# Issue order inside a pooled attention and a gated two-layer product: what is queued behind what, on VectorE, TensorE and the DMA queue

## The chip, the cores and the metric

The kernel runs on one core of one Trainium2 chip. The metric is the device time of one execution in microseconds. The core has a matrix engine (TensorE; PE in the profile, its weight loads are PEld), VectorE (DVE), ScalarE (ACT), GpSimd (POOL) and SyncE (SP), which in this kernel issues nearly all DMAs. Each engine works through its own instructions in the order in which they stand in the program.

## The reference, cut to what matters

```python
# q, k, v: 8 batches x 8 heads x 576 tokens x 64;  w_in: 512 x 2048;  w_out: 2048 x 512; all float32
k_p = k.reshape(B, H, 72, 8, D).mean(axis=3)          # eight keys become one
v_p = v.reshape(B, H, 72, 8, D).mean(axis=3)
scores = q @ k_p.T / sqrt(D)
attn = exp(scores - max(scores))                      # softmax over 72 pooled keys
attn = attn / (attn.sum(-1) + 1e-9)
x = (attn @ v_p), heads side by side                  # 4608 tokens x 512
h = x @ w_in                                          # 4608 x 2048
g = h * clip(h + 3, 0, 6) / 6
out = g @ w_out                                       # 4608 x 512
```

## The kernel before, in words

**Precision.** Products are made in a fast 32-bit format. Each operand is split into a high part (a copy into that format, by ScalarE) and a low part (the rest, a subtraction by VectorE), and each product is three matmuls: high by high, high by low, low by high.

**Blocks.** The 4608 tokens are cut into blocks of 512, 256 and ten times 384. The first four blocks run plainly (`Step`): for each of 16 slices f of the middle dimension, `h()` makes twelve matmuls (line 813), ScalarE and VectorE make the gate and its two parts (lines 821 to 833), and `out()` multiplies them with `w_out` two steps later (line 843). In VectorE's work on a step the last instruction is `lo()` (line 833).

**Super blocks.** The other eight blocks are taken in pairs by `super_block`, four in all. Its first half makes h for two blocks at once with seven products in the place of eight. `N1` lists 56 operations (pair i of slices, product o from 1 to 7), six matmuls of 384 columns each (line 1041). Each reads a pre-added piece of `w_in`, streamed from DRAM in chunks of two operations into a ring of four (`next_w`, tile ws, line 938), and a pre-added part of x: x1 to x7, made by `x_ops` of four quarters of x (b11, b21 of the first block, b12, b22 of the second). Results of one pair gather in the PSUM banks X, Y and Z; between products ScalarE keeps a copy (`keep`, line 1019), VectorE adds (`plus`, line 1014), and `gate` follows (lines 1008 and 1009). The last operation of a pair (o = 4) needs the sum that `plus` takes after o = 7 from the same bank. The second half makes out: for 16 slices f, `split_g` makes the two parts of g (lines 1025 and 1026) and six token tiles t take three matmuls each (line 1086), with `w_out` streamed slice by slice into a ring of four (`next_w2`, tile ws2, line 944; the profile calls both rings ws, this one from w2d). The sums of t = 0 to 5 stand in the banks o0, h0, o2, o1, h1, o3; all but o3 also serve the h half, and o3 is one of three that the attention uses meanwhile.

**The sources of both streams** are written by the kernel while blocks 2 and 3 run: `sums_of` adds quarters of `w_in` (line 909, then lines 914 to 916) in one buffer and stores them (line 918); `plain_of` stores what needs no addition through `store` (line 921, 24 stores of 256 KB and 16 of 512 KB).

**Attention** for later blocks is cut into steps that are dealt out among the products (`Paced.slot`). `scores` (lines 443 to 485) makes one tile's scores for four heads and divides them on GpSimd into a tile a (line 479); `transposes` (lines 549 to 572) turns it round; `av` (lines 619 to 621) multiplies it with the pooled values and writes x. `block_steps` puts the transposes of a tile behind the scores of `TLAG` = 3 later ones; tile a has two buffers. Side steps load k and v for a later batch and sum over eight keys (lines 243 and 362, reductions on VectorE). A super block deals out the attention of the two blocks after next, 36% of the steps in its first half and the rest in its second, up to f = 10; from f = 11 the steps of `x_ops` follow, in the order in which `x_ops` returns them.

**Order.** All instructions are first written down in program order. Up to the fourth step of block 1 the order on each engine is then set by hand (`ORDER`; `window` holds both ends of that stretch). Behind it a planner decides: it goes through a model of the machine and gives each engine, among the instructions that are ready there, the one that was written down first. An edge made by `behind(a, b)` costs no semaphore on the chip; it only keeps the planner from placing a before b. `after_products`, the only such edge of this kind before, names as b the last TensorE instruction written down so far, and is called behind the reductions of k and v, the two additions of line 909, the stores of line 921 and the loads of ws2.

Of the kernel before, what the change touches and what calls it, by code (L numbers as in the profile page):

```python
# [17 lines left out]
P = 128  # L18
# [8 lines left out]
TLAG = 3  # L27
# [62 lines left out]
def attention_moe_kernel(  # L90
# [72 lines left out]

    def after_products():

        if len(window) == 2:
            behind(traced[-1], next(i for i in reversed(traced) if i.engine == mybir.EngineType.PE).name)

# [64 lines left out]
    def prep_k(b, p):  # L233

        two = b == 0
        if not two:
            ks = pool.tile([P, 1, SP], F32, name="ksum", bufs=1)
        elif p % 2 == 0:
            ks = ksum[p // 2] = piece(0, 2 * SP).rearrange("p (i s) -> p i s", i=2)
        else:  # L240
            ks = ksum[p // 2]
        i = p % 2 if two else 0
        nc.vector.tensor_reduce(
            out=ks[:, i], in_=kraw.pop((b, p)).rearrange("p (s o) -> p s o", o=POOL), axis=AX.X, op=ALU.add
        )
        after_products()
        if i == two:

            scale = 1.0 / (POOL * D**0.5)
            for h in range(2):  # L250
                rows = slice(h * D, (h + 1) * D)
                nc.scalar.mul(kbds[b % 2][rows, p - i : p + 1, h * SP : (h + 1) * SP], ks[rows], scale)
# [99 lines left out]
    def prep_v(b, p):  # L352


        if p == 0:
            if b not in W:
                place_v(b)
            sums = ring("vsum")[:, : (NPAIR + NG) * D]
            vsum[b] = sums.rearrange("p (c d) -> p c d", d=D)
        n = P if p < NPAIR else 3 * REM  # L360
        vs, st = vsum[b], vraw.pop((b, p))
        nc.vector.tensor_reduce(  # L362
            out=vs[:n, p], in_=st[:n, : POOL * D].rearrange("p (o d) -> p d o", o=POOL), axis=AX.X, op=ALU.add
        )
        after_products()
        if p == NPAIR - 1:
            place_heads(b, vs[:, :NPAIR])
        elif p == NPAIR + NG - 1:
            place_rest(b, vs[:, NPAIR:])
# [50 lines left out]
    class Scores:  # L420
# [49 lines left out]
        def divide(self, engine):  # L470

            e, sm = self.e, self.sm
            if self.a is None:
                self.a = pool.tile([P, 4 * D], F32, name="a", bufs=2)
                if self.g == 0:
                    rests[self.tile] = pool.tile([P, NG, 2 * REM], F32, name="ar", bufs=2)
                self.rest = rests[self.tile][:, self.g]
# [167 lines left out]
    def block_steps(j):  # L645
# [12 lines left out]
        for t in tiles_of[j]:  # L658
            pre = loads_behind(t)
            for g in range(NG):  # L660
                steps.append((pre, lambda t=t, g=g: scores(j, t, g), "scores", [x[0] for x in t]))
                pre = []
                todo.append((t, g))
                if len(todo) > TLAG:
                    turn()
# [134 lines left out]
    class Step:  # L800
# [30 lines left out]
        def lo(self):  # L831
            self.glo = early.tile([P, max(BLOCKS)], F32R, name="glo", bufs=3)[:, : self.n]
            nc.vector.tensor_tensor(out=self.glo, in0=self.g, in1=self.ghi.bitcast(F32), op=ALU.subtract)

        def out(self, slot=no_slot):
# [67 lines left out]
    def sums_of(i, h):  # L903
# [4 lines left out]
        for r, w in enumerate(pair_of(i)):  # L908
            nc.vector.tensor_tensor(
                out=q[:, 2 * r : 2 * r + 2], in0=w[:, 0, :, half], in1=w[:, 1, :, half], op=ALU.add  # L910
            )
            after_products()
        for to, a, b, how in ((0, 0, 2, ALU.subtract), (2, 2, 3, ALU.add), (3, 3, 0, ALU.subtract), (1, 1, 3, ALU.subtract)):
# [6 lines left out]
    def store(to, src):  # L920
        nc.sync.dma_start(to, src)
        after_products()

# [11 lines left out]
    def next_w(n):  # L935
        while (m := len(loaded)) <= n // CHUNK + AHEAD and m < len(supers) * len(w_dram):
            loaded[m] = late[0].tile([P, CHUNK, 2, 2 * P], F32R, name="ws", bufs=NSTREAM)
            nc.sync.dma_start(loaded[m].bitcast(F32), w_dram[m % len(w_dram)])
        return loaded[n // CHUNK][:, n % CHUNK]

    def next_w2(n):
        while (m := len(loaded2)) <= n + 3 and m < len(supers) * NF:
            loaded2[m] = late[1].tile([P, 2, DM], F32R, name="ws2", bufs=4)
            nc.sync.dma_start(loaded2[m].bitcast(F32), w2_dram[m % NF])
            after_products()
        return loaded2[n]
# [3 lines left out]
    def x_ops(j):  # L950
# [24 lines left out]
        def middle():  # L975
# [5 lines left out]
        return (  # L981
            mix(middle, b22, b12, ALU.subtract)
            + split(1, b11)
            + mix(b12, b12, b11, ALU.subtract)
            + split(2, b21)
            + mix(b11, b11, middle, ALU.add)
            + split(7, middle)
            + split(5, b12)
            + mix(b21, b21, b11, ALU.subtract)
            + split(6, b11)  # L990
            + split(4, b21)
            + split(3, b22)
        )

    def super_block(n, j, first_att, second_att):
# [9 lines left out]
        def gate(src, i, k):  # L1005
# [4 lines left out]
                out=g_of[i][:, k], in0=r, scalar=GSCALE, in1=src, op0=ALU.min, op1=ALU.mult  # L1010
            )

        def plus(i, k, ps, kept):
# [8 lines left out]
        def split_g(f):  # L1022
            g = g_of[f // 2][:, f % 2 :: 2]
            hi, lo = (late[1].tile([P, 2, HALF], F32R, name=m, bufs=3) for m in ("ghi2", "glo2"))
            nc.scalar.copy(hi, g)  # L1025
            nc.vector.tensor_tensor(out=lo, in0=g, in1=hi.bitcast(F32), op=ALU.subtract)  # L1026
            parts[f] = [t.rearrange("p h t -> p (h t)") for t in (hi, lo)]

        for m, (i, o) in enumerate(N1):
# [27 lines left out]
            elif o == 4:  # L1057
                gate(ps, i, 1)
        paced.upto(len(paced.steps))

# [7 lines left out]
        for f in range(NF):  # L1068
# [3 lines left out]
            for t in range(NT2):  # L1072
# [11 lines left out]
                for cols, pos in sums[t]:  # L1084
                    for k, (l, r) in enumerate(products):
                        nc.tensor.matmul(pos, l, w[:, r, cols], start=f == 0 and k == 0, stop=end and k == 2)  # L1086
                if not end:
                    continue
# [240 lines left out]
    for n, j in enumerate(supers):  # L1329
        last = n == len(supers) - 1  # L1330
        att = [] if last else att_steps(j + 2) + att_steps(j + 3)
        cut = int(0.36 * len(att))
        super_block(n, j, att[:cut], att[cut:])
# [46 lines left out]
```

## Time and profile before

| | |
|---|---|
| median of 3 runs | 915.89 us (912.76 to 915.96) |
| the profiled execution's own time | 916.45 us |
| its span, first to last instruction | 914.7 us |
| TensorE busy | 889.2 us, 97% |
| VectorE, ScalarE, GpSimd busy | 569.7, 515.6, 82.9 us |
| granted TensorE clock, mean | 0.996 |
| bytes moved by DMA | 172.63 MB, 189 GB/s on average |

The profile shows one execution. Block 0 ends and block 1 begins at about 128 us, block 2 begins at 188, block 3 at 266, and the four super blocks at 355, 500, 639 and 781 us; their second halves begin at about 417, 561, 702 and 838 us. In a timeline row the first number is the start in microseconds from the span's beginning, the second how long the merged instructions took together, and a bracket at the end gives how long the engine had been idle before and what ended that. Rows merge equal instructions (x18 is eighteen), and a row can overlap the next, since matmuls are pipelined. In a row of DMA issues the duration is that of issuing; the time to landing stands apart.

### The profile page before, as it was taken

The numbers are of one execution on the slowest core, as the hardware profiler recorded it, in microseconds if no ns is written. First come the engines' busy times: TensorE is split into PE (matmuls) and PEld (weight loads), VectorE is DVE, ScalarE is ACT, GpSimd is POOL, SyncE is SP. The second block draws the span as 40 slices with busy tenths as digits, with TensorE's granted clock in tenths as the row PEclk, the third lists the DMA queues.
The fourth block names the chain that finished last, engine by engine and source line by source line (L and its number), as shares of the span: only waits on it lengthen the run. The fifth ranks groups of instructions, "written<-read, shape, count | busy, mean of one in ns | idle before, by whom it ended". The sixth has DMA issues, their size and how long they took to land.

```text
span 914.7 us, 14060 instructions
## 1 busy us (share of the span) xinstructions
PE 889.2 (97%) x4760; PEld 797.4 (87%) x4760; DVE 569.7 (62%) x1183; ACT 515.6 (56%) x1473; POOL 82.9 (9%) x168
## 2 busy tenths in 40 slices
PE   7899999999999998999999999999999999899998
PEld 7788889998889987899888999888999888899887
DVE  5999855587876786466744845665665543744321
ACT  5898766666557565446534854554854443644221
POOL 4100002111102011000100300110200010000000
PEclk9999999999999999999999999999999999999999
DMA  9970205246659546886745666764777543576333
GB/s 292 392 270 1 79 15 160 66 155 195 210 161 340 179 144 199 287 265 204 236 162 175 231 213 215 239 200 156 235 230 224 184 127 117 197 230 217 115 121 110
DMA packets 93527, 172.63 MB, mean 189 GB/s; under 512 B 12048, under 2 KB 50704, under 8 KB 93456
## 3 DMA queue, kind: packets, MB, share of 16 engines
q1 hardware_dynamic: 93312, 171.74, 56.8%
q8 instruction: 38, 0.62, 0.3%
q14 instruction: 33, 0.27, 0.1%
q10 hardware_dynamic: 144, 0.00, 0.0%
HBM read 139.20 MB, written 32.51 MB: 188 GB/s over the span
## 4 chain that ended last, share of the span: by engine, by line
PE 86%; DVE 6%; DMA 4%; ACT 1%; SPq 1%; issue 1%; DVEq 0%; ACTq 0%
PE psx L1086 29%; PE psx L1041 24%; PE psh L813 12%; PE pso L843 12%; PE psa L619 3%; PE psa L443 3%; DMA ws<-wd 2%; PE psa L549 1%; DMA wd<-wq 1%; DMA stage<-v_l 1%; DVE x L960 1%; SPq L918 1%; PE psa L320 1%; DVE vsum L362 1%; DVE wq L916 0%
## 5 line engine op out<-in xcount | busy, mean ns | idle before, releaser
L1041 PE MATMUL psx<-x,ws 128*128 128x384 f32 x1344 | 249.4, 339 | 5.7 <-DMA ws<-wd 2.3
L1041 PEld LDWEIGHTS psx<-x,ws 128*128 128x128 f32 x1344 | 233.9, 189 | 11.5 <-ACT c L1019 2.5
L1086 PE MATMUL psx<-ws,ghi 128*128 128x512 f32 (+1 forms) x800 | 239.2, 386 | 4.8 <-DVE g L1009 2.6
L1086 PEld LDWEIGHTS psx<-ws,ghi 128*128 128x128 f32 x800 | 146.0, 188 | 31.8 <-DVE g L1009 3.5
L1086 PE MATMUL psx<-ws,glo 128*128 128x512 f32 (+1 forms) x400 | 149.0, 386 | 0.3 <-DVE glo L1026 0.3
L813 PE MATMUL psh<-xhi,w 128*128 128x384 f32 (+2 forms) x520 | 146.1, 339 | 0.3 <-DVE g L825 0.3
L843 PE MATMUL pso<-w,ghi 128*128 128x512 f32 x384 | 120.1, 399 | 0.0
L1026 DVE TENSOR_TENSOR glo<-g,ghi 128x768 fp32r<-128x768 f32 x64 | 61.5, 965 | 74.0 <-ACT ghi L1025 68.7
L813 PEld LDWEIGHTS psh<-xhi,w 128*128 128x128 f32 x520 | 93.4, 188 | 7.4 <-DVE g L825 0.5
L451 ACT ACTIVATE e<-psa,mx 128x72 f32<-128x72 f32 x256 | 78.8, 328 | 22.5 <-DVE mx L447 19.2
L1008 ACT ACTIVATE r<-g,small 128x384 f32<-128x384 f32 x96 | 55.6, 616 | 58.6 <-DVE g L1014 58.4
L1025 ACT CAST ghi<-g 128x768 fp32r<-128x768 f32 x64 | 53.1, 838 | 62.5 <-PE psx L1086 60.6
L1086 PEld LDWEIGHTS psx<-ws,glo 128*128 128x128 f32 x400 | 75.1, 188 | 14.6 <-DVE glo L1026 1.2
L813 PE MATMUL psh<-xlo,w 128*128 128x384 f32 (+2 forms) x260 | 87.3, 336 | 0.0
L479 POOL TENSOR_TENSOR a<-e,sm 128x256 f32<-128x256 f32 x60 | 41.6, 695 | 403.7 <-DVE sm L468 326.5
L843 PEld LDWEIGHTS pso<-w,ghi 128*128 128x128 f32 x384 | 68.5, 188 | 10.0
L1014 DVE TENSOR_TENSOR g<-psx,c 128x384 f32<-128x384 f32 x96 | 52.7, 554 | 35.5 <-PE psx L1041 32.8
L843 PE MATMUL pso<-w,glo 128*128 128x512 f32 x192 | 73.8, 397 | 0.0
L1019 ACT COPY c<-psx 128x384 f32<-128x384 f32 x96 | 43.4, 486 | 39.9 <-PE psx L1041 39.1
L1009 DVE SCALAR_TENSOR_TENSOR g<-r,psx 128x384 f32<-128x384 f32 x32 | 17.7, 553 | 62.7 <-ACT r L1008 62.5
L451 ACT ACTIVATION_READ_ACCUMULATOR e<-psa,mx 128x1 f32 x256 | 54.7, 214 | 0.0
L1009 DVE SCALAR_TENSOR_TENSOR g<-r,g 128x384 f32<-128x384 f32 x96 | 50.5, 557 | 5.5 <-ACT r L1008 5.4
(120 smaller groups left out, 1191.7 us busy)
## 6 DMA issues: line engine op xcount, KB each, us to landing
ws<-wd SPq DMA_DIRECT2D x112, 512.0 KB, 4.2
ws<-w2d SPq DMA_DIRECT2D x64, 512.0 KB, 3.4
out<-o SPq DMA_DIRECT2D x35, 256.0 KB, 3.1
raw<-w_in_l SPq DMA_DIRECT2D x16, 512.0 KB, 8.7
raw<-w_out_l SPq DMA_DIRECT2D x16, 512.0 KB, 9.5
w2d<-w SPq DMA_DIRECT2D x16, 512.0 KB, 4.0
wd<-wq SPq DMA_DIRECT2D x64, 128.0 KB, 2.0
kst<-k_l SPq DMA_DIRECT2D x28, 288.0 KB, 4.2
```

The lines of the kernel that those rows point to most:

```text
L451: nc.scalar.activation(self.e[:, h], self.ps[:, h], AF.Exp, bias=self.mx[:, h : h + 1], accum_out=self.sm[:, h : h + 1])
L479: engine.tensor_tensor(out=self.a[:, : 4 * D].rearrange("p (h s) -> p h s", h=4), in0=e[:, :, :D], in1=sm[:, :, None].broadcast_to([P, 4, D]),
L813: nc.tensor.matmul(self.ps, l[f][:, c, :], r[:, c, :], start=c == 0 and i == 0, stop=c == NCC - 1 and i == 2)
L843: nc.tensor.matmul(pos, l, r, start=f == 0 and i == 0, stop=f == NF - 1 and i == 2)
L1008: nc.scalar.activation(r, src, AF.Relu, bias=half_low, scale=GSCALE / (6.0 * WSCALE))
L1009: nc.vector.scalar_tensor_tensor(out=g_of[i][:, k], in0=r, scalar=GSCALE, in1=src, op0=ALU.min, op1=ALU.mult)
L1014: nc.vector.tensor_tensor(out=g_of[i][:, k], in0=ps, in1=kept, op=ALU.add)
L1019: nc.scalar.copy(c, ps)
L1025: nc.scalar.copy(hi, g)
L1026: nc.vector.tensor_tensor(out=lo, in0=g, in1=hi.bitcast(F32), op=ALU.subtract)
L1041: nc.tensor.matmul(ps, w[:, l, c * P : (c + 1) * P], t[:, r, c], start=o in (1, 2, 5) and c == 0 and k == 0, stop=c == 1 and k == 2, skip_ ...
L1086: nc.tensor.matmul(pos, l, w[:, r, cols], start=f == 0 and k == 0, stop=end and k == 2)
```

## The change

Seven edits, all of them on order, pacing and one buffer:

- `mark()` notes for its engine the instruction just written down: VectorE's `lo()` of a step, the gate and the low part of `split_g`, and on the DMA queue each load of ws.
- `after_mark()` replaces `after_products()`: the reductions, the additions of line 909 and the loads of ws2 are put behind the latest marked instruction of their own engine, and no longer behind one of TensorE. `store` has no edge any more.
- The first matmul of each token tile's sum for out is put behind the last matmul for h of the same super block.
- From block 3 on, transposes follow two later scores in place of three.
- Tile a has three buffers in place of two.
- `x_ops` returns its steps in the order x1, x2, x5, x6, x3, x7, x4, with each addition ahead of the part that needs it first, in place of x1, x2, x7, x5, x6, x4, x3.
- 45% of a super block's attention steps go into its first half, in place of 36%.

```diff
-    def after_products():
-
-        if len(window) == 2:
-            behind(traced[-1], next(i for i in reversed(traced) if i.engine == mybir.EngineType.PE).name)
+    marks = {}
+
+    def mark():
+        marks[traced[-1].engine] = traced[-1].name
+
+    def after_mark():
+
+        if len(window) == 2 and traced[-1].engine in marks:
+            behind(traced[-1], marks[traced[-1].engine])
...
-        after_products()        # prep_k (243), prep_v (362), sums_of (909), next_w2 (944)
+        after_mark()
...
-                self.a = pool.tile([P, 4 * D], F32, name="a", bufs=2)
+                self.a = pool.tile([P, 4 * D], F32, name="a", bufs=3)
...
-                if len(todo) > TLAG:
+                if len(todo) > (TLAG if j < 3 else 2):
                     turn()
...
             nc.vector.tensor_tensor(out=self.glo, in0=self.g, in1=self.ghi.bitcast(F32), op=ALU.subtract)
+            mark()
...
     def store(to, src):
         nc.sync.dma_start(to, src)
-        after_products()
...
             nc.sync.dma_start(loaded[m].bitcast(F32), w_dram[m % len(w_dram)])
+            mark()
...
-            mix(middle, b22, b12, ALU.subtract)
-            + split(1, b11)
+            split(1, b11)
+            + split(2, b21)
+            + mix(middle, b22, b12, ALU.subtract)
             + mix(b12, b12, b11, ALU.subtract)
-            + split(2, b21)
+            + split(5, b12)
             + mix(b11, b11, middle, ALU.add)
+            + split(6, b11)
+            + split(3, b22)
             + split(7, middle)
-            + split(5, b12)
             + mix(b21, b21, b11, ALU.subtract)
-            + split(6, b11)
             + split(4, b21)
-            + split(3, b22)
...
                 out=g_of[i][:, k], in0=r, scalar=GSCALE, in1=src, op0=ALU.min, op1=ALU.mult
             )
+            mark()
...
             nc.vector.tensor_tensor(out=lo, in0=g, in1=hi.bitcast(F32), op=ALU.subtract)
+            mark()
...
+        last_h = next(i for i in reversed(traced) if i.engine == mybir.EngineType.PE).name
         paced.upto(len(paced.steps))
...
                         nc.tensor.matmul(pos, l, w[:, r, cols], start=f == 0 and k == 0, stop=end and k == 2)
+                        if f == 0 and k == 0:
+                            behind(traced[-1], last_h)
...
-        cut = int(0.36 * len(att))
+        cut = int(0.45 * len(att))
```

More of the change, by code (lines that the diff above doesn't have):

```diff
@@ L364, in prep_v @@
         )
-        after_products()
+        after_mark()
         if p == NPAIR - 1:
@@ L911, in sums_of @@
             )
-            after_products()
+            after_mark()
         for to, a, b, how in ((0, 0, 2, ALU.subtract), (2, 2, 3, ALU.add), (3, 3, 0, ALU.subtract), (1, 1, 3, ALU.subtract)):
@@ L921, in store @@
         nc.sync.dma_start(to, src)
-        after_products()
     def plain_of(i, n):
@@ L944, in next_w2 @@
             nc.sync.dma_start(loaded2[m].bitcast(F32), w2_dram[m % NF])
-            after_products()
+            after_mark()
         return loaded2[n]
```

## The prediction, made before the changed kernel was run

> **What bounds the kernel now.** I read the page's head, then stretches by stage, then TensorE's timeline where a stretch shows it idle.
>
> ```profile
> span 914.7 us, 14060 instructions
> PE 889.2 (97%) x4760; PEld 797.4 (87%) x4760; DVE 569.7 (62%) x1183; ACT 515.6 (56%) x1473; POOL 82.9 (9%) x168
> ```
>
> TensorE is the bound: 889.2 of 914.7 us, and no edit adds or removes a matmul. What order can win is TensorE's lost time alone. Where it lies:
>
> ```profile
> core 0: us, PE busy (x) PEld busy (x) DVE busy (x) ACT busy (x) POOL busy (x), PEclk, DMA share, GB/s
> ...
> 188.00:266.00 78.00, 76.34 (x416) 68.51 (x415) 60.19 (x151) 42.78 (x140) 8.29 (x17) 1.00 0.59 186
> 266.00:355.00 89.00, 88.04 (x477) 79.74 (x476) 69.99 (x179) 58.60 (x200) 13.26 (x27) 1.00 0.60 196
> 355.00:417.00 62.00, 57.59 (x310) 55.13 (x311) 35.69 (x66) 29.78 (x61) 0.00 (x0) 0.97 0.83 283
> ...
> 781.00:838.00 57.00, 54.55 (x315) 52.97 (x314) 34.25 (x63) 30.84 (x61) 0.00 (x0) 1.00 0.67 219
> 838.00:914.70 76.70, 71.56 (x360) 61.33 (x358) 19.82 (x27) 17.69 (x26) 0.00 (x0) 1.00 0.36 119
> ```
>
> Up to the fourth step of block 1 the hand-written order holds and no edge is set. Behind it two stretches stand out: the h half of the first super block (62.00 less 57.59: 4.4 us idle, and the only one with a lower clock, 0.97) and that of the last (2.45 us). Blocks 2 and 3 together lose 2.6 us. Of the last 76.7 us, 5.1 are idle, the wait for the final store among them, which stays.
>
> **Products for out behind those for h.** TensorE at the first super block's start, then the pitch when nothing is in its way (the chain of waits):
>
> ```profile
> 355.02 6.51 PE L1041 MATMUL psx<-x,ws 128*128 128x384 f32 x36 [0.67 <-ACT o L848]
> 362.94 0.70 PE L1086 MATMUL psx<-ws,ghi 128*128 128x512 f32 x2 [1.41 <-DMA ws<-w2d]
> 364.81 3.88 PE L1041 MATMUL psx<-x,ws 128*128 128x384 f32 x12 [1.17 <-DMA ws<-wd]
> 368.53 0.40 PE L1086 MATMUL psx<-ws,glo 128*128 128x512 f32 x1
> ...
> 372.94 0.62 PE L1086 MATMUL psx<-ws,ghi 128*128 128x512 f32 x2
> 373.63 0.49 PE L1086 MATMUL psx<-ws,glo 128*128 128x512 f32 x1
> 374.96 0.73 PE L1086 MATMUL psx<-ws,ghi 128*128 128x512 f32 x2 [0.84 <-ACT ghi L1025]
> 375.95 0.51 PE L1086 MATMUL psx<-ws,glo 128*128 128x512 f32 x1 [0.26 <-DVE glo L1026]
> ```
>
> ```profile
> 376.46 20.92 PE psx L1041 x120
> ```
>
> The pitch is 20.92/120 = 0.174 us for 384 columns; for 512 it is about 0.23 (372.94 to 373.63, three starts). Products for out (line 1086), for the one token tile whose bank the h half leaves free, stand among the seventh to seventeenth operation for h. Each waits for its own gate parts or its load, and the products for h queue behind it. Lost, start to start: 355.02 + 36 x 0.174 = 361.28 to 362.94, 1.66; 363.40 to 364.81, 1.41; then twelve matmuls in 3.72 us where 2.09 would do, 1.63, the dip of the clock; 373.40 to 373.63, 0.23; 373.86 to 374.96, 1.10; 375.42 to 375.95, 0.53. Together 6.56 us. The new edge takes all these products out of the h half.
>
> What is late next is the stream: the eighth operation's chunk. The DMA queue here, and that chunk in the chain of waits:
>
> ```profile
> 357.69 0.48 SPq L944 DMA_DIRECT2D ws<-w2d  x1
> 358.27 0.38 SPq L938 DMA_DIRECT2D ws<-wd  x1
> ```
>
> ```profile
> 358.27 6.41 DMA ws<-wd
> ```
>
> ```profile
> ws<-wd SPq DMA_DIRECT2D x112, 512.0 KB, 4.2
> ```
>
> It took 6.41 us (4.2 in the median) behind 512 KB of ws2. The four loads of ws2 stand here because their edge points at a TensorE instruction that the planner ran early; the new edge puts them behind the load of ws that was written down last, forty operations into the half. Without them the chunk can be issued at 357.7 and land 4.2 to 6.4 us later, 361.9 to 364.1, against 361.28 when it is wanted: 0.6 to 2.8 us of wait remain. I take 1.2, nearer the median. The same four loads then meet the ws stream at a place where it runs 6.3 us ahead (three chunks of two operations of 1.04 us); four times 512 KB at the 283 GB/s of this stretch are 7.4 us, so 0 to 1.5 us come back, 0.5 taken. Term: -6.6 + 1.2 + 0.5 = **-4.9** (-6.6 to -2.3).
>
> The clock fell to half (1.63 us more) after idle times of 1.66 and 1.41 us around two matmuls. [...]
>
> At the end of an h half the same products are filler, and that is lost:
>
> ```profile
> 846.05 2.25 PE L1041 MATMUL psx<-x,ws 128*128 128x384 f32 x12
> ...
> 852.22 1.21 PE L1041 MATMUL psx<-x,ws 128*128 128x384 f32 x6
> 854.75 0.73 PE L1086 MATMUL psx<-ws,ghi 128*128 128x512 f32 x2 [1.32 <-DVE g L1009]
> ```
>
> ```profile
> 848.33 0.56 DVE L1014 TENSOR_TENSOR g<-psx,c 128x384 f32<-128x384 f32 x1 [0.48 <-PE psx L1041]
> 575.91 0.73 PE L1086 MATMUL psx<-ws,ghi 128*128 128x512 f32 x2 [0.59 <-DVE g L1009]
> 716.65 0.73 PE L1086 MATMUL psx<-ws,ghi 128*128 128x512 f32 x2 [0.67 <-DVE g L1009]
> ```
>
> Operation 55 ends its six matmuls' issue at 846.05 + 12 x 0.174 = 848.13; operation 56 needs line 1014's sum, done at 848.89, so it can start at about 848.95. Now 18 products for out fill that and more; afterwards the 0.82 us are open, in four super blocks 3.3 us (less where attention fills three of them: 0.8 to 4). Against that, the products for out that follow operation 56 now wait for its gate, because all others have been spent: 1.32, 0.59 and 0.67 idle, 2.6 us. Afterwards the four tiles on other banks come first (12 x 0.23 = 2.8 us, more than the gate's wait). Term: +3.3 - 2.6 = **+0.7** (-1.8 to +1.4).
>
> **Sums behind VectorE's marks, a third tile a, transposes earlier, 45%, x parts by use.** These meet at the start of the last super block, which waits for x.
>
> ```profile
> 780.50 0.34 PE L619 MATMUL psa<-ahi,vlo 128*128 128x384 f32 x1
> ...
> 780.85 3.30 PE L1041 MATMUL psx<-x,ws 128*128 128x384 f32 x18
> 784.70 1.51 PE L1041 MATMUL psx<-x,ws 128*128 128x384 f32 x7 [0.54 <-DVE g L1014]
> 786.97 1.32 PE L1041 MATMUL psx<-x,ws 128*128 128x384 f32 x6 [0.76 <-DVE x L960]
> 788.86 2.18 PE L1041 MATMUL psx<-x,ws 128*128 128x384 f32 x11 [0.57 <-ACT c L1019]
> ...
> 791.61 2.70 PE L1041 MATMUL psx<-x,ws 128*128 128x384 f32 x14 [0.57 <-ACT c L1019]
> ```
>
> Attention's last product runs at 780.50, though its step was dealt out by f = 10, and x's additions and splits run only then, beside the products that need them. Lost: 783.98 to 784.70, 0.72; 785.92 to 786.97, 1.05; 788.01 to 788.86, 0.85; 790.77 to 791.61, 0.84. Together 3.5 us. Why attention is late:
>
> ```profile
> 691.66 0.89 SPq L263 DMA_DIRECT2D vst<-vr_l  x2
> ```
>
> ```profile
> 716.51 1.05 DVE L362 TENSOR_REDUCE vsum<-vst 96x64 f32<-96x512 f32 x1
> ```
>
> ```profile
> 753.48 0.61 POOL L479 TENSOR_TENSOR a<-e,sm 128x256 f32<-128x256 f32 x1 [5.59 <-PE psa L551]
> ```
>
> The last sum of v runs 24 us after its data were asked for, in the out half, because its edge points at a TensorE instruction of attention that is itself late; behind a gate of the h half it runs before 702. A division waits 5.59 us for transposes to free one of the two tiles a; a third tile, and one score less between, take that away. Either is enough to bring the last product, and the 9 us of additions and splits behind it, ahead of 780. The order by use counts only where that fails: x5 no longer waits behind x7, which takes the 1.05 away. Term: **-3.3** (-3.5 to -1.0). The 45% moves three or four steps into an h half whose VectorE and ScalarE are half busy (35.69 and 29.78 of 62): no cost.
>
> **Blocks 2 and 3.** The additions of line 909 wait in VectorE's queue for their buffer:
>
> ```profile
> DVE wq L909 <- DMA wd<-wq: 11.5, 10, 3.1
> ```
>
> That is 11.5 us of VectorE between 217 and 353; behind `lo()` they come later, when the buffer is free. It reaches TensorE only by the idle 2.6 us. The stores, without an edge, may all go out when the hand-written order ends (a rival, below). I take **0** (-2.6 to the rival's price).
>
> **Sum.** -4.9 + 0.7 - 3.3 + 0 = -7.5 us, against the profiled execution's 916.45 (span 914.7, 1.75 around it), which is 0.56 above the median of the runs: **909.0 us**, 0.8% faster.
>
> **Rivals.**
>
> *The stores flood the queue (slower).* 24 x 256 KB and 16 x 512 KB are 14.7 MB; now they go out one by one:
>
> ```profile
> 171.66 0.55 SPq L222 DMA_DIRECT2D qt<-q_l  x1
> ...
> 184.00 1.13 SPq L921 DMA_DIRECT2D wd<-w  x2
> ```
>
> ```profile
> raw<-w_out_l SPq DMA_DIRECT2D x16, 512.0 KB, 9.5
> ```
>
> The hand-written order ends about four of block 1's sixteen steps behind its start: 128 + 4 x 60/16 = 143 us. At the 283 GB/s of the busiest stretch above the flood lasts 52 us, to 195. A load of q like that at 171.66 would come 10 us late behind three quarters of the stores (143 + 39 = 182) and 24 behind all, and scores already placed on TensorE would hold what stands behind them. That a burst delays is seen in the weights' first loads: 9.5 us to landing against the 4.2 of equally large ones above. It decides from the point where a load is later than the planner supposed; at the middle, 17 us, once, the time is 909.0 + 17 = 926. Against it: the planner may see the same contention and place the scores later, and block 3 has from 188 to 266 to spare. 0.13. [...]
>
> *The gain is given back (no change).* The order of all engines is planned anew behind the hand-written part; waits like the 1.17 and the 0.84 above arise elsewhere, and each term comes out at its poor end: -2.3 - 1.0 + 1.4 = -1.9, 914.5 us. For it speaks that the planner placed the products above where they stall. 0.22.
>
> *More goes.* Attention fills the ends of the h halves, blocks 2 and 3 lose nothing: each term at its good end: -6.6 - 1.8 - 3.5 - 2.6 = -14.5, 902 us. Against it: some wait for the stream is left by any reckoning above. 0.12.
>
> *It doesn't do what it says:* the planner may still place the sums late; then the last super block's 3.3 stay, 912.3; that lies in the forecast's own range.
>
> **Numbers.** Forecast 0.53, its own range 905 to 913.5; no change 0.22, flood 0.13, more 0.12. A measurement of this kernel tells about 0.5% from no change, 4.6 us: faster is below 911.3, slower above 920.5. Faster: three quarters of 0.53, 0.12 and 0.03 of the no-change case, 0.55. Slower: 0.13. Same: 0.32. The range 903 to 919 leaves out about half of "more" and most of the flood.
>
> **What would show it.** The h half of the first super block: no line 1086 before its last line 1041, granted clock 1.00, TensorE's loss below 2 us. Each half's last six matmuls of line 1041 behind an idle time near 0.8 us on line 1014. The last line 619 before 775 us of the old time scale and no wait on lines 960 or 1019 at the last super block's start. Stores of line 921 from 143 us on with q loads behind them would be the flood. A wait of over 3 us on ws<-wd, or idle times over 3 us in blocks 1 to 3, would make the forecast wrong.

## The result and the profile after

The changed kernel takes **909.95 us** (median of 20 runs, 905.60 to 913.64) against 916.48 for the kernel before measured beside it (912.76 to 917.96): a ratio of 0.9931, 95% interval 0.9918 to 0.9944. The forecast was 909.0.

The sum came out right and most of its terms did not. A profiled execution can lie off its kernel's median (this one took 912.95 us, that of the run with the stores' edge back 921.72 against 916.63), so the lines show the places and the medians of the experiments the sizes. Its head, and the stretches that were shown of the kernel before (us from the span's start, busy time and number of instructions of each engine, granted clock, share of the DMA engines, GB/s):

```profile
span 911.2 us, 14053 instructions
PE 887.9 (97%) x4760; PEld 798.0 (88%) x4760; DVE 572.9 (63%) x1183; ACT 517.1 (57%) x1473; POOL 82.4 (9%) x168
```

```profile
188.00:266.00 78.00, 77.91 (x429) 71.17 (x428) 61.54 (x153) 47.66 (x158) 9.23 (x20) 1.00 0.49 141
266.00:355.00 89.00, 87.88 (x481) 80.10 (x480) 68.46 (x181) 58.06 (x200) 13.64 (x27) 1.00 0.41 124
355.00:417.00 62.00, 57.29 (x307) 55.00 (x307) 41.34 (x80) 36.11 (x89) 2.04 (x5) 0.94 0.88 297
...
781.00:838.00 57.00, 56.12 (x319) 54.73 (x318) 29.24 (x54) 28.88 (x56) 0.00 (x0) 1.00 0.73 242
838.00:911.20 73.20, 68.70 (x349) 58.46 (x347) 17.17 (x22) 14.79 (x20) 0.00 (x0) 1.00 0.32 108
```

The first super block's h half, where 4.9 us were to be won, idles 4.71 us of its 62 (4.41 before), at a clock of 0.94 (0.97 before). Two other places are better: block 2 idles 0.09 us of 78 (1.66 before), and the last super block's start 0.88 of 57 (2.45 before). One is worse: the third super block's h half, 639 to 702 us, idles 1.80 us (0.46 before). TensorE's timeline shows what took the place of the old stalls; no line 1095 (products for out) stands in any h half:

```profile
355.54 2.33 PE L1049 MATMUL psx<-x,ws 128*128 128x384 f32 x12
359.71 5.45 PE L1049 MATMUL psx<-x,ws 128*128 128x384 f32 x21 [1.84 <-DMA ws<-wd]
...
406.52 1.32 PE L1049 MATMUL psx<-x,ws 128*128 128x384 f32 x6
408.78 0.76 PE L448 MATMUL psa<-kbd,qt 128*128 128x144 f32 x4 [0.93 <-ACT x L626]
411.34 3.46 PE L1049 MATMUL psx<-x,ws 128*128 128x384 f32 x12 [1.80 <-DMA ws<-wd]
...
779.69 17.85 PE L1049 MATMUL psx<-x,ws 128*128 128x384 f32 x102
...
839.82 1.31 PE L1049 MATMUL psx<-x,ws 128*128 128x384 f32 x6 [0.65 <-DVE g L1021]
```

Both waits of 1.8 us are for a chunk of ws; the first is for the chunk of the ninth operation, which the prediction calls the eighth (in both kernels eight operations, 48 products, stand ahead of it). Behind each the products run slower: 21 in 5.45 us and 12 in 3.46, where 0.174 us each would make 3.65 and 2.09; the granted clock was 0.69 and 0.63 in these two stretches. At 779.69 stand 102 products without a gap, where the kernel before stopped four times. What released the products at 411.34 stands in the chain of waits, with the load that it waited for; ahead of it, SP's queue:

```profile
401.19 2.17 SPq L950 DMA_DIRECT2D ws<-w2d  x4
403.46 0.42 SPq L943 DMA_DIRECT2D ws<-wd  x1
```

```profile
403.46 7.83 DMA ws<-wd
```

Four loads of ws2 go out in one burst, and the chunk behind them takes 7.83 us to land, against 4.3 in the median (the row below). The third thing that is new is the stores: all 40 leave within 41 us once the hand-written order has ended, with one load of q (at 152.28) and three of v between them, and the next load of q behind the last:

```profile
148.71 1.53 SPq L927 DMA_DIRECT2D wd<-w  x3
...
188.38 1.44 SPq L927 DMA_DIRECT2D w2d<-w  x2
189.92 1.03 SPq L227 DMA_DIRECT2D qt<-q_l  x1
```

```profile
ws<-wd SPq DMA_DIRECT2D x112, 512.0 KB, 4.3
```

### The profile page after: what moved, and what is told of

Read it like the earlier page. It is cut to its first block, busy times and chain, and to the rows that moved or that the text cites. A ratio compares the mean times of both kernels' runs of the same rounds, so it can differ in the third digit from the quotient of the medians.

```text
span 911.2 us, 14053 instructions
## 1 busy us (share of the span) xinstructions
PE 887.9 (97%) x4760; PEld 798.0 (88%) x4760; DVE 572.9 (63%) x1183; ACT 517.1 (57%) x1473; POOL 82.4 (9%) x168
## 4 chain that ended last, share of the span: by engine, by line
PE 78%; DMA 8%; DVE 8%; ACT 2%; SPq 1%; issue 1%; DVEq 0%; ACTq 0%
PE psx L1095 29%; PE psx L1049 20%; PE psh L818 11%; PE pso L849 11%; DMA ws<-wd 5%; PE psa L448 3%; PE psa L624 3%; DMA stage<-q_l 2%; DMA wd<-wq 2%; PE psa L554 1%; DVE x L966 1%; ACT e L456 1%; DVE wq L915 1%; SPq L924 1%; DVE wq L920 1%
## 5 line engine op out<-in xcount | busy, mean ns | idle before, releaser
L1095 PE MATMUL psx<-ws,ghi 128*128 128x512 f32 (+1 forms) x800 | 242.7, 384 | 0.0
L1095 PE MATMUL psx<-ws,glo 128*128 128x512 f32 (+1 forms) x400 | 153.2, 383 | 0.0
L1033 DVE TENSOR_TENSOR glo<-g,ghi 128x768 fp32r<-128x768 f32 x64 | 63.5, 993 | 102.4 <-ACT ghi L1032 98.6
L484 POOL TENSOR_TENSOR a<-e,sm 128x256 f32<-128x256 f32 x60 | 39.7, 662 | 490.3 <-DVE sm L473 423.3
L826 ACT ACTIVATE g<-psh,small 128x384 f32<-128x384 f32 (+2 forms) x65 | 37.8, 581 | 29.7 <-PE psh L818 16.3
```

The source lines that it names most:

```text
L484: engine.tensor_tensor(out=self.a[:, : 4 * D].rearrange("p (h s) -> p h s", h=4), in0=e[:, :, :D], in1=sm[:, :, None].broadcast_to([P, 4, D]),
```

## The experiments

Each is measured in five rounds against the kernel before. All but three start from the changed kernel; those three start from the kernel before.

| kernel | us, median (runs) | ratio to before, 95% interval | granted clock, mean of the runs |
|---|---|---|---|
| changed kernel | 909.95 (20) | 0.9931, 0.9918 to 0.9944 | 0.9973 |
| changed, products for out free | 906.64 (6) | 0.9884, 0.9862 to 0.9906 | 0.9987 |
| changed, loads of ws2 apart | 904.87 (4) | 0.9875, 0.9857 to 0.9893 | 0.9978 |
| changed, both of these | 903.95 (6) | 0.9872, 0.9849 to 0.9895 | 0.9983 |
| changed, stores' edge back | 916.63 (12) | 1.0007, 0.9991 to 1.0023 | 0.9933 |
| changed, sums' edges back | 909.54 (6) | 0.9929, 0.9905 to 0.9954 | 0.9980 |
| changed, pace back | 914.91 (12) | 0.9986, 0.9970 to 1.0002 | 0.9970 |
| changed, pace back, loads of ws2 apart | 911.61 (12) | 0.9944, 0.9927 to 0.9961 | 0.9989 |
| changed, x order back | 909.58 (6) | 0.9929, 0.9900 to 0.9957 | 0.9970 |
| both of these, ring of nine | 907.36 (6) | 0.9908, 0.9883 to 0.9933 | 0.9988 |
| before, stores free | 915.38 (12) | 0.9995, 0.9981 to 1.0010 | 0.9969 |
| before, products for out behind | 914.12 (12) | 0.9981, 0.9965 to 0.9996 | 0.9963 |
| before, stores free and new pace | 907.57 (6) | 0.9911, 0.9882 to 0.9939 | 0.9997 |

"Pace" stands for three edits together: three tiles a instead of two, transposes two scores behind instead of three in the last blocks, 45% instead of 36% of the attention steps in the h half. They were not taken apart.

The kernel before, run beside each group, took 915.92 to 916.70 us in the median at a mean clock of 0.9979 to 0.9985, so differences between rows are good to about 1 us. TensorE bounds the kernel, so 0.001 of clock is put at 0.9 us below, an estimate from its 888 us of busy time.

### Products for out, free again

```diff
-                        if f == 0 and k == 0:
-                            behind(traced[-1], last_h)
```

> The changed kernel without the edge that puts the products for out behind those for h; all else as changed. Theory P (the prediction's): the edge is worth some 4 us in the first super block's h half, so the time rises from 910 to about 914 and line 1095 stands among the first seventeen operations for h again. Theory S (from the profile after): the edge only moved the loss from stalled products to the wait for the ws stream, and took filler away from the h halves; without it the time is 908 to 911, the waits on ws<-wd shrink from 7 us in total to about 3, and the products for out, whose ws2 is now loaded late, cannot come early in the first super block anyway.

906.64 us, below even theory S's 908 to 911: the edge costs the changed kernel some 3.3 us (4.3 by the ratios). The same stretch of the profile, and TensorE's wait for the stream over the whole span, first of this kernel and then of the changed one (us in total, times, longest):

```profile
355.00:417.00 62.00, 59.76 (x333) 56.73 (x332) 41.67 (x82) 36.25 (x91) 2.04 (x5) 1.00 0.90 306
```

```profile
PE psx L1049 <- DMA ws<-wd: 4.2, 7, 1.1
```

```profile
PE psx L1049 <- DMA ws<-wd: 6.6, 9, 1.8
```

Without products for out between them, operations of 1.04 us ask for 512 KB every 2.09 us, 250 GB/s, and the waits for the stream are 6.6 us in place of 4.2. The timed runs' clock, 0.9973 against 0.9987, is some 1.3 us more. The stalls that the edge was to cure do not return when it is taken out: no idle time ahead of line 1095 stands in this stretch, nor does it in the kernel that has the new pace and never had the edge (below).

### The four first loads of ws2, apart

```diff
+    def first_w2(n):
+        while len(loaded2) < n:
+            loaded2[len(loaded2)] = late[1].tile([P, 2, DM], F32R, name="ws2", bufs=4)
+            nc.sync.dma_start(loaded2[len(loaded2) - 1].bitcast(F32), w2_dram[len(loaded2) - 1])
+            after_mark()
...
-            if n == 0 and i == NPR - 2 and o == 1:
-                next_w2(0)
+            if n == 0 and i >= NPR - 4 and o == 1:
+                first_w2(i - NPR + 5)
```

> The changed kernel with the first four loads of ws2 issued one each at the beginning of pairs 4 to 7 of the first super block, in place of four in a row at pair 6. Theory S: the four in a row are what the h half waits for at 409 us (1.96 us and the half clock behind it); apart, both go, 2 to 4 us less, 906 to 908, and no wait over 1 us on ws<-wd behind 370 us in the first super block. Theory P (the prediction's 0.5 us for it): 909.5, no difference that can be measured.

904.87 us, below theory S's 906 to 908: the burst costs 5 us, ten times what the prediction took for it. The place at 411 us of the changed kernel, now, and its stretch:

```profile
410.37 2.35 PE L1055 MATMUL psx<-x,ws 128*128 128x384 f32 x12 [0.23 <-DMA ws<-wd]
```

```profile
355.00:417.00 62.00, 58.24 (x333) 56.55 (x332) 44.25 (x85) 38.68 (x96) 2.05 (x4) 1.00 0.92 318
```

One wait of 1.12 us for ws remains, at 384 us. In the two profiled executions 6.4 of the 8.0 us between them lie from the wait for the ninth operation's chunk to the first product for out (359.71 to 424.10 us in the changed kernel, 358.29 to 416.27 now), so the place is shown. The split is not: the timed runs' clock, 0.9973 against 0.9978, is some 0.5 us of the 5.

### Both

The two diffs above in one kernel.

> The changed kernel with both earlier edits: no edge on the products for out, and the first four loads of ws2 one at a time at the four pairs before. If the two take away different losses (the edge: the stream of ws without slack; the burst of loads: the stall at 409 us), the gains of 3.3 and 5.1 us add up and it takes 901.5 to 903. If both cure one and the same stall of the first super block, it takes 904 to 905.5, no better than the loads apart alone. If the products for out, free again, stand where their gates are late, as in the kernel before, 906 to 908.

903.95 us, the lowest median here, but its interval covers all of that of the loads apart (0.9857 to 0.9893). The gains of 3.3 and 5.1 us do not add up to 8.4; the measured 6.0 is nearer to two cures of one stall, and what the second adds is not settled.

### The stores' edge back

```diff
     def store(to, src):
         nc.sync.dma_start(to, src)
+        after_products()
```

> The changed kernel with the stores of line 927 put behind the last TensorE instruction again, as before the change. Theory F: the stores' early burst (149 to 190 us) is what blocks 1 and 2 gain from (3.5 us shorter in the profile after), since it is out of the way of the wq stores and the loads later; spread again, the time rises by 2 to 3 us to 912 or 913. Theory V: blocks 1 and 2 gain by the place of the sums on VectorE; the time stays within 1 us of 910, and the loads of q come at 172 us again without any gain.

916.63 us, more than theory F's 912 or 913: one line takes the whole gain away. The stretches of this kernel; the first two carry 195 and 199 GB/s, as before the change (186 and 196), instead of 141 and 124:

```profile
188.00:266.00 78.00, 76.31 (x416) 69.08 (x415) 61.09 (x154) 43.77 (x145) 8.60 (x18) 1.00 0.62 195
266.00:355.00 89.00, 87.99 (x478) 80.18 (x476) 66.19 (x168) 57.89 (x197) 12.08 (x23) 1.00 0.61 199
355.00:417.00 62.00, 54.68 (x293) 52.63 (x293) 42.01 (x80) 34.23 (x78) 2.53 (x5) 0.94 0.82 268
...
781.00:838.00 57.00, 53.53 (x290) 51.66 (x289) 27.40 (x50) 26.57 (x51) 0.00 (x0) 0.97 0.70 232
```

How the stores reach TensorE can be followed on three engines at the first super block's start, VectorE, GpSimd, TensorE:

```profile
346.22 0.76 DVE L920 TENSOR_TENSOR wq<-w 128x256 f32<-128x256 f32 x2 [2.10 <-DMA wd<-wq]
...
353.58 0.76 DVE L920 TENSOR_TENSOR wq<-w 128x256 f32<-128x256 f32 x2 [1.51 <-DMA wd<-wq]
```

```profile
355.25 0.61 POOL L489 TENSOR_TENSOR a<-e,sm 128x256 f32<-128x256 f32 x1 [3.31 <-DVE sm L478]
```

```profile
355.92 0.44 PE L559 MATMUL psa<-ident,a 128*128 128x128 f32 x2 [1.93 <-POOL a L489]
357.24 0.44 PE L559 MATMUL psa<-ident,a 128*128 128x128 f32 x2 [0.88 <-POOL a L489]
...
360.61 3.89 PE L1055 MATMUL psx<-x,ws 128*128 128x384 f32 x11 [2.35 <-ACT c L1032]
```

The weight sums (line 920) wait in VectorE's queue for their one buffer to be stored; they last until after 353 us, where attention's reciprocals already stand behind them, the divisions on GpSimd wait for those, and TensorE for the divisions; the 2.35 us at 360.61 come by way of ScalarE, whose copy stands behind the parts that it makes from those transposes. Of the 62 us there 7.3 are idle. In the changed kernel the last of these sums (line 915 there) starts 7.7 us earlier, and no product of TensorE waits for a division:

```profile
345.89 0.76 DVE L915 TENSOR_TENSOR wq<-w 128x256 f32<-128x256 f32 x2 [1.36 <-DMA wd<-wq]
```

Whether the stores' place moves the sums through the queue itself or through the planner's order was not singled out, and this path is not the whole price. The last super block's h half idles 3.47 us (0.88 in the changed kernel), all of it in three waits for ws (1.80, 1.05 and 0.62). And the twelve timed runs had a clock of 0.991 to 0.994, 0.9933 in the mean, against 0.9973: some 3.6 of the 6.7 us.

### The stores' edge gone, in the kernel before

```diff
     def store(to, src):
         nc.sync.dma_start(to, src)
-        after_products()
```

> The kernel before with one line less: the stores of the weight parts have no edge; everything else, the sums' place, the pace of attention, the order of x and of the products, is as before. The run that put the stores' edge back into the changed kernel took the whole gain away (916.6). Theory F, the early burst by itself shortens blocks 1 and 2 and lets VectorE's sums of weights end before the first super block: 909.5 to 912, with all stores out by 190 us and blocks 1 and 2 together some 3 us shorter. Theory I, it takes the other edits too (the burst only mends what the edge on the products for out and the third a would break): 914.5 to 917. Theory R, the flood that the prediction's rival saw, hidden in the changed kernel only by the others: 920 and more.

915.38 us, as theory I said: alone it is worth nothing that can be measured. The flood is there (348 GB/s from 140 to 191 us, with TensorE busy in 51.00 of the 51 us), but the two stalls that the prediction described stay where they were; TensorE's timeline:

```profile
362.21 0.70 PE L1085 MATMUL psx<-ws,ghi 128*128 128x512 f32 x2 [1.31 <-DMA ws<-w2d]
365.37 8.08 PE L1040 MATMUL psx<-x,ws 128*128 128x384 f32 x36 [1.94 <-DMA ws<-wd]
...
784.99 1.34 PE L1040 MATMUL psx<-x,ws 128*128 128x384 f32 x6 [0.77 <-DVE x L959]
```

### The pace back

```diff
-                self.a = pool.tile([P, 4 * D], F32, name="a", bufs=3)
+                self.a = pool.tile([P, 4 * D], F32, name="a", bufs=2)
-                if len(todo) > (TLAG if j < 3 else 2):
+                if len(todo) > TLAG:
-        cut = int(0.45 * len(att))
+        cut = int(0.36 * len(att))
```

> The changed kernel with two tiles a, transposes three scores behind and 36% as before; stores, sums, x order and the edge on the products stay changed. The prediction's term says that these, with the sums, hold the last super block's 3.3 us: 912 to 913.5, with a wait on x or on attention's last product back at its start. Rival: the early stores already let attention run ahead, and the pace is worth nothing: 909 to 910.5.

914.91 us, more than the prediction's term allows, and not by that term: the last super block starts with 150 products in a row. The largest stall is another, behind the burst of ws2 (the same view, TensorE's timeline):

```profile
410.88 7.94 PE L1049 MATMUL psx<-x,ws 128*128 128x384 f32 x30 [4.13 <-DMA ws<-wd]
...
782.05 26.17 PE L1049 MATMUL psx<-x,ws 128*128 128x384 f32 x150
```

### The pace back, with the loads of ws2 apart

The diff above and that of the loads apart in one kernel.

> The changed kernel with attention's pace of before and with the first four loads of ws2 one at a time at the four pairs before. With the old pace and the four loads in one burst it took 914.9, and TensorE waited 4.3 us for one chunk of ws behind the burst, where no attention lay between the products. Theory B, the pace counts only through that stall (attention lies elsewhere beside the burst): with the loads apart the pace is worth nothing, 904.5 to 906.5. Theory A, the pace is worth its 5 us by itself (sums and x ahead of the super blocks' starts): 909 to 911.

911.61 us against 904.87 with the new pace. So the pace is worth 6.7 us (6.3 by the ratios) without any burst, and theory B falls. Stretches of this kernel:

```profile
188.00:266.00 78.00, 77.16 (x421) 69.85 (x420) 62.03 (x156) 46.20 (x154) 9.59 (x20) 1.00 0.48 139
266.00:355.00 89.00, 86.64 (x470) 78.41 (x469) 67.75 (x175) 58.10 (x200) 14.23 (x27) 1.00 0.38 113
...
636.00:706.00 70.00, 67.56 (x402) 66.25 (x401) 48.53 (x105) 44.62 (x134) 5.71 (x12) 0.98 0.69 225
```

The same stretches with the new pace idle 0.09, 1.00 and 0.74 us; here 0.84, 2.36 and 2.44, and the third at a lower clock. In it, VectorE waits for a load of v that attention needs at once, and TensorE behind it for a sum in VectorE's queue (VectorE's and TensorE's timelines):

```profile
678.12 1.07 DVE L367 TENSOR_REDUCE vsum<-vst 96x64 f32<-96x512 f32 x1 [1.75 <-DMA vst<-vr_l]
```

```profile
682.90 7.40 PE L1055 MATMUL psx<-x,ws 128*128 128x384 f32 x32 [1.99 <-DVE g L1027]
```

These idle times differ by 3.8 us; where the other 2.9 lie was not singled out.

### The stores and the pace alone

In the kernel before, the store's line without its edge, and the pace of the changed kernel.

> The kernel before with two parts of the change alone: the stores without their edge, and attention's pace (three tiles a, transposes two scores behind in the last blocks, 45%). The sums' place, the order of x and the products for out stay as before. The stores alone gave 915.4, the change without them 916.6, the change without the pace 914.9. Theory J, the gain needs these two together and nothing else: 905.5 to 908.5, as the changed kernel without the edge on the products for out (906.6). Theory K, a third part (sums or x) is needed as well: 912 to 916.

907.57 us from these edits alone. Theory J holds: without either of the two the changed kernel has no gain to speak of (916.63 and 914.91), and together they suffice. The sums' place, the x order and the edge on the products for out can all stay as before. The pace alone in the kernel before was not run; the nearest to it is the changed kernel with the stores' edge back. From the kernel with the stores alone this one differs by the pace only, and the stalls shown there at 362.21 us (products for out) and 784.99 (x) are not in it. The first super block's h half and the last one's start in this kernel:

```profile
355.00:417.00 62.00, 59.48 (x343) 57.71 (x342) 43.75 (x87) 39.05 (x103) 3.84 (x8) 1.00 0.90 300
781.00:838.00 57.00, 56.25 (x323) 54.74 (x322) 27.79 (x52) 26.89 (x52) 0.00 (x0) 1.00 0.66 214
```

### The sums' place, and the x order

```diff
-        after_mark()
+        after_products()
```

(at the sums of k and v and at the additions of weights), and in the other run x's parts in the old order:

```diff
-            split(1, b11)
-            + split(2, b21)
-            + mix(middle, b22, b12, ALU.subtract)
+            mix(middle, b22, b12, ALU.subtract)
+            + split(1, b11)
...
+            + split(2, b21)
...
-            + split(6, b11)
-            + split(3, b22)
...
```

> The changed kernel with the reductions of k and v and the additions of line 915 put behind the last TensorE instruction again, as before the change. Theory V: blocks 1 and 2 lose 2 to 3 us, and the last sums of v run in the out half again, so that x is late for the last super block (3 us): 913 to 916. Theory F: the place of the sums is worth nothing in blocks 1 and 2, and the third tile a and the earlier transposes are enough for x: 909.5 to 911.

> The changed kernel with x's differences and splits in the old order. The prediction says that the order counts only where attention ends too late for it: 909 to 910.5, no wait on x at any super block's start. Rival: the last super block's start is short of x whatever attention does, and the 1.05 us per start come back: 911 to 914.

909.54 and 909.58 us against 909.95: neither place can be told from no change. The last super block starts with 136 and with 102 products without a gap.

### Products for out behind, in the kernel before

```diff
+        last_h = next(i for i in reversed(traced) if i.engine == mybir.EngineType.PE).name
...
+                        if f == 0 and k == 0:
+                            behind(traced[-1], last_h)
```

> The kernel before with one part of the change alone: the products for out may only start behind the last product for h of their super block. It is the prediction's largest step by itself, in the kernel for which it was worked out. Prediction's step: -4.9 at the first super block's start and +0.7 at the ends of the h halves, so 911.5 to 912.5. Theory S (from the changed kernel, which is 3.3 us faster without this edge): the h halves lose the products for out as filler, the stream of ws has no slack left and the four loads of ws2 come in one burst, 917 to 920. Theory Z, the stall of the kernel before that goes and the new ones are worth the same: 914.5 to 917.

914.12 us, 0.9981 (0.9965 to 0.9996): a gain of 0.04% to 0.35%, less than the prediction's step. By the median it is just under theory Z's 914.5, by the ratio (914.7 for 916.48) within it. Its profile shows why the step gave less, and that the edge also does what the prediction put down to the sums and the pace (TensorE's timeline):

```profile
356.76 6.54 PE L1041 MATMUL psx<-x,ws 128*128 128x384 f32 x36 [0.82 <-ACT o L848]
366.48 8.08 PE L1041 MATMUL psx<-x,ws 128*128 128x384 f32 x36 [3.18 <-DMA ws<-wd]
...
781.00 26.56 PE L1041 MATMUL psx<-x,ws 128*128 128x384 f32 x150
```

The stall at the first super block is now one wait of 3.18 us for the stream, and the clock drops behind it (36 products in 8.08 us instead of 6.3). The timed runs agree: a clock of 0.9963 against 0.9979 of the kernel before beside them, some 1.5 us. The last super block's start is clean.

### A finer ring

```diff
-CHUNK, NSTREAM, AHEAD, NC, NREL = 2, 4, 3, 6, 3
+CHUNK, NSTREAM, AHEAD, NC, NREL = 1, 9, 8, 5, 3
```

> The kernel without the edge on the products for out and with the loads of ws2 apart (903.95), with the ring of ws in single operations, nine buffers of 256 KB and eight loads ahead, in place of four of 512 KB and three ahead (for the room one tile fewer of kept values). Theory S, the stream's lead is short by under one operation: the waits for ws at the first super block's start (2.7 us) and behind (1.4, 1.0, 0.4 us) shrink to under 2 us in all, 900 to 902.5. Theory Q, the queue's rate sets it: twice as many loads of half the size move no more bytes in the time, 903 to 905. Theory K, the kept values then wait for a tile: 906 or more.

907.36 us against 903.95, with intervals that overlap a little: none of the three theories as written. The time is theory K's, its cause is not: ScalarE's copies of kept values (line 1032) wait for TensorE's products alone, not for a tile. The waits for the stream do shrink (first the kernel without this edit, then this one), and half loads land in 3.5 us instead of 4.2:

```profile
PE psx L1055 <- DMA ws<-wd: 5.1, 5, 2.6
```

```profile
PE psx L1055 <- DMA ws<-wd: 1.5, 1, 1.5
```

```profile
188.00:266.00 78.00, 76.64 (x417) 68.82 (x417) 60.80 (x151) 46.84 (x157) 9.23 (x20) 1.00 0.46 133
266.00:355.00 89.00, 85.82 (x458) 76.41 (x457) 65.14 (x172) 52.87 (x183) 12.25 (x24) 1.00 0.40 119
```

The loss lies ahead of the first super block, in blocks 2 and 3, which idle 1.36 and 3.18 us (0.09 and 1.18 without the edit). Why the order planned there comes out worse stays open.

## Why the prediction was right, point by point

**Right in the sum (909.95 against 909.0, and inside 903 to 919), by terms that miss in opposite directions.** Two terms were to carry it, -4.9 at the first super block and -3.3 at the last one. What carries it are the stores, for which the prediction took 0, together with the pace: these two alone gain some 8 us. That the terms add up to within 1 us of the measured time is luck.

- *Products for out behind those for h, -4.9.* This step failed. The stall that it described was real, and it goes: by itself the edge gains some 2 us in the kernel before, and that profile's first super block is no better (57.22 us busy of 62, against 57.59). Beside the other edits it costs 3.3 us. Two terms in it were mis-sized. First, the wait for the eighth operation's chunk: 1.2 us taken, 1.84 measured in the changed kernel and 3.18 with the edge alone. Second, the burst of four loads of ws2: 0.5 us taken from 0 to 1.5, 5 us measured. The reckoning of the burst, 7.4 us of transfer against a lead of 6.3, was not far off (the chunk took 7.83 us and the wait was 1.80); what it left out is the drop of the clock behind this wait, to 0.63 in the profiled execution. The 0.93 us of the scores ahead of it are a wait for ScalarE's copy of x (line 626), which the prediction did not have either; with the loads apart it is gone. In the timed runs the clock is only some 0.5 us of the burst's 5, and the rest was not taken apart. The lower bound of -6.6 also leaves out the 0.6 us of wait that the same working says remain at least.
- *The clock.* Behind the waits of 1.84 and 1.80 us the products ran slower; the stretch's clock of 0.94 over 62 us is 3.7 us. But the same wait at the same place, 1.84 us in the kernel with the x order back, was followed by 12 products in 2.32 us, full speed, and one of 1.69 us in the kernel with stores and pace alone by 94 in 16.53:

```profile
359.33 2.32 PE L1049 MATMUL psx<-x,ws 128*128 128x384 f32 x12 [1.84 <-DMA ws<-wd]
```

```profile
359.75 16.53 PE L1040 MATMUL psx<-x,ws 128*128 128x384 f32 x94 [1.69 <-DMA ws<-wd]
```

  With the stores' edge back even 2.43 us (at 418 us) were followed by 12 products in 2.37. So in this kernel a wait of 1.7 to 2.4 us is to be priced with and without the drop (1.8 us more for the 21 products, 1.4 for the 12). The prediction's sum took its waits of 1.2 and 0.5 us at full clock, an estimate of its author: the wait of 1.12 us with the loads apart lies in a stretch at a clock of 1.00, but no run shows up to what length that holds. The clock fell behind 1.80 and 1.84 us in one execution and did not behind 1.69, 1.84 and 2.43 us in three others.
- *Ends of the h halves, +0.7.* Better than that. The wait for line 1021 appears as described, 0.65 us in the last super block, but attention fills most of the other ends, and the waits of 1.32, 0.59 and 0.67 us are gone. Over the whole span 1.1 us remain, so the term is 1.1 - 2.6 = -1.5, within its bounds:

```profile
PE psx L1049 <- DVE g L1021: 1.1, 2, 0.7
```

- *Sums, third a, transposes, 45%, x by use, -3.3.* The effect came, the four stops at the last super block's start are gone. The cause was half wrong. The sums, which the prediction named first, are worth nothing, nor is the x order, as it said. The stops also go with the edge on the products alone, and with stores and pace alone. The pace, which it priced only there, is worth 5.0 us in the changed kernel and 6.7 with the loads apart, part of it in blocks 2 and 3 and in the third super block.
- *Blocks 2 and 3, 0.* Failed: here the stores' part was missed. Putting their edge back costs 6.7 us. That the additions of weights wait in VectorE's queue "reaches TensorE only by the idle 2.6 us" left out the next stage: with the stores' edge and the new pace they end in the first super block's start, and there attention's divisions wait behind them. That is a part of the 6.7; the lower clock, some 3.6 us, and the waits for ws in the last super block are others.
- *The rival of the flood.* It described the burst rightly, stores from 148.7 to 189.8 us with loads of q behind. Its price did not fall due: TensorE did not stop between 140 and 191 us, and the point from which it decides, a load later than supposed, was not reached. Its 10 and 24 us take it that a load waits for all stores ahead of it, which no run shows by itself; the loads of q at 152.28 and 189.92 us landed 6.2 and 5.1 us after their issue, against 3.1 for that at 171.66 us before the change. It saw the 50 us of the burst and not the 160 behind them, in which the queue carries less (141 and 124 GB/s instead of 186 and 196). That this is by itself a gain is not shown: in the kernel with the stores alone blocks 2 and 3 carry 137 and 116 GB/s and idle 1.60 and 1.76 us, more than before the change.
- *What was to show it.* No line 1095 in the h half: right. Clock 1.00 and a loss below 2 us there: wrong. The last h products behind some 0.8 us: 0.65. Attention's last product before 775 us: right, 767.03. No wait on x at the last super block: right. No wait over 3 us on ws: right, 1.8 at most.

## What to carry to other kernels

An idle engine's cause can lie one stage further back than the wait that ends last: with the stores' edge back a chain of sums, which stores through the same queue, ran 7.7 us later and into the next stage, where divisions and then TensorE stood behind it. The stores' edit gained nothing alone and 6.7 us in the changed kernel, so a part that shows nothing by itself should be tried beside the others before it is dropped. Filler between products that stream their weights was also slack for the stream (4.2 us of waits with it, 6.6 without): whoever moves it out should first look how far ahead the loads run, and spread other loads over that stretch instead of issuing them in one burst. And the granted clock of the timed runs belongs beside their times: here it holds over half of what the stores' edge costs.

## What the hardware showed that was not expected

The stores of 14.7 MB were issued within 41 us beside loads of attention. The stretch carried 344 GB/s, where the prediction had reckoned with 283, and TensorE lost nothing:

```profile
140.00:191.00 51.00, 51.00 (x326) 46.63 (x325) 29.04 (x77) 31.05 (x118) 9.63 (x21) 1.00 0.95 344
```

And waits of 1.7 to 2.4 us were followed by a lower clock in one execution (0.69 behind 1.84 us) and by none in another (12 products in 2.32 us behind 1.84); what decides between them no run here shows. Within the changed kernel the three timed runs at a clock of 1.000 took 905.60 to 908.33 us, the eight at 0.996 908.53 to 912.95.
